# Banded attention and a SiLU layer on one core: batch 2's strided heads turned by VectorE, a subtraction on GpSimd, fewer identity products

## The chip, the cores and the metric

The kernel runs on one core of one Trainium2 chip. Its metric is the device time of one execution, in microseconds (us). A profiled execution also gives a span, from the first to the last instruction, and a trace of every instruction of TensorE (PE), VectorE (DVE), ScalarE (ACT), GpSimd (POOL) and the sync engine's DMA queue (SP).

## The reference

There are 8 batches, 8 heads, 576 positions and 64 numbers per head. Heads 0 to 3 attend to the last 32 positions, heads 4 to 7 to every fourth of the last 128. The result goes, token by token, through two matrices with SiLU between them.

```python
B, H, S, D = q.shape                      # 8, 8, 576, 64
scores = np.matmul(q, k.transpose(0, 1, 3, 2)) / np.sqrt(D)
rel = np.arange(S)[:, None] - np.arange(S)[None, :]
plain = (rel >= 0) & (rel < 32)
dilated = (rel >= 0) & (rel < 128) & (rel % 4 == 0)
scores = np.where(plain or dilated by head, scores, -1e9)
attn = np.exp(scores - scores.max(-1, keepdims=True))
attn = attn / (attn.sum(-1, keepdims=True) + 1e-9)
x = np.matmul(attn, v)                    # to (B * S, H * D) = (4608, 512)
h = x @ w_in                              # (4608, 2048)
out = (h * sigmoid(h)) @ w_out            # (4608, 512), float32
```

## The kernel before

Everything is cut by batch `b` and by kind of head `z`: `z = 0` for the four plain heads, `z = 1` for the four strided ones, whose positions are sorted into four classes (position modulo 4) so that each class is again a plain band. A band is computed in blocks of 32 queries by 64 keys, four heads side by side on the 128 partitions. The steps for one `(b, z)` are these.

- `load_qk` brings q and k on GpSimd's DMA queue into a pair of tiles `n0`, `n1` (a pool with two buffers each, so batch `b + 2` uses the buffers of batch `b`). `load_one` loads rows of many positions; `load_squares` loads in blocks of 32 by 32 or 32 by 96, in more and smaller pieces. For `b >= DT` (3) the squares are used.
- q and k must lie with the 64 numbers of a head on the partitions. Below `DT`, `transpose` (L249) does this with TensorE, into PSUM tiles `t`, and DVE and ACT copy them out (`to_classes` for `z = 1`). From `DT` on, `turn_qk` (L294) does it with one DVE stream transpose each for k and q, from the squares.
- `scores` runs the small products (`score`, `score_class`, `score_turned`) into PSUM, `masked` (L374) adds scale and mask into `ms`, `reduce_max` (L441) gives the negated maxima `nm`. Each half `hi` of the blocks has tiles of its own.
- `exps` (L521) runs on ACT, one pair of instructions for each block of 64 columns: an exponential with the maximum as bias, and the read of its sum into `l`. Where `shift` has already subtracted the maxima, one wide exponential (L510) does it, and `total` (L529) sums on DVE.
- `normal` (L540 to L543) divides on DVE into `pn`, `turned` (L559) turns 32 by 32 blocks into `pt`, `values` (L590) multiplies with `vw`, the v tile, into four PSUM tiles `x`, and `finish` (L622, L624) copies those, as f16, into `xT`.
- `layer1` (L672) multiplies `xT` with `w_in` in 16 steps `f`, each ended by a SiLU on ACT (L680) into `gT`. `layer2` (L741) multiplies `gT` with `w_out` in tiles of 128 tokens, 16 products each, and `store` (L726) copies a tile `o` to SBUF, on DVE, and sends it out on SP's queue.

ScalarE loads a table (1.28 us) whenever it goes from exponentials to SiLU or back.

The order on each engine is the order in which the program issues its instructions; each engine runs its own in that order. `plan_of(b)` lists what of the attention of later batches is issued at which step of batch `b`'s layers: steps 0 to 15 stand ahead of `layer1`'s 16 values of `f`, and from 16 on each step is a quarter (4 products) of a `layer2` tile, so that tile `x` has steps `16 + 4x` to `19 + 4x`. A tile's `store` is issued after its last quarter. `later` lists normalising, values and finish of one `(b, z)` at the steps it is given; during batch `b` the normalising, values and finish of batch `b + 1` are issued.

PSUM has the pool `big` (two buffers, for `h`, `o` and batch 0's scores) and the pool `ps` (four, for all else). An `o` tile waits until the tile two before it has been copied out.

Batch 0 comes ahead of the loop and is done in two parts of its tokens (`part`), each with `scores0`, `values0`, `finish0` and, in the loop, `layer1_part` (L697). `warm` (L632) issues products of the identity with itself, 256 columns wide, whose result is overwritten.

Of the kernel before, what the change touches and what calls it, by code (L numbers as in the profile page):

```python
# [25 lines left out]
DT = 3  # L26
# [3 lines left out]
def kernel(  # L30
# [61 lines left out]
    def tiles_qk(b):  # L92

        for which in (0, 1):
            t = nat.tile([P, GN[0] * QB + GN[1] * GW], F16, tag=f"n{which}", name=f"n{which}_{b}")
            if b >= DT:
                qk[b, 0, which] = t[:, 0 : GN[0] * QB].rearrange("p (g e) -> p g e", e=QB)
                qk[b, 1, which] = t[:, GN[0] * QB :].rearrange("p (g e) -> p g e", e=GW)
                continue
            t = t[:, 0 : 2 * sum(URS) * D].rearrange("p (u d) -> p u d", d=D)  # L100
            u0, u1 = 2 * URS[0], 2 * (URS[0] + URS[1])
            qk[b, 0, which] = t[:, 0:u0].rearrange("p (h u) d -> p h u d", h=2)
            qk[b, 1, which] = t[0 : 2 * UPS[1] if b == 0 else P, u0:u1].rearrange("p (h u) d -> p h u d", h=2)

# [33 lines left out]
    def load_qk(b):  # L138

        tiles_qk(b)  # L140
        if b >= DT:
            for z in (0, 1):
                for which in (1, 0):
                    load_squares(b, z, which)
            return
        for z in (1, 0) if b == 1 else (0, 1):
            for which in (1, 0):
                load_one(b, z, which)
# [182 lines left out]
    def score(b, h, j, dst, start=True):  # L331

        if b >= DT:
            score_turned(b, 0, h, 0, j, dst)
            return
        a = att(b)
        hp = h // 2
        o = (h + hp) % 2 * D
        r = slice(o, o + D)
        nc.tensor.matmul(  # L340
            dst[h * QB : h * QB + QB],
            a["qT"][r, hp, j * QB : j * QB + QB],
            keys(b, a["kT"][r, hp, j * QB : j * QB + KB]),
            start=start,
            stop=True,
            skip_group_check=not start,
        )

    def score_class(b, h, c, j, dst, start=True):

        if b >= DT:
            score_turned(b, 1, h, c, j, dst)
            return
# [93 lines left out]
    def scores(b, z, half=None):  # L447
# [13 lines left out]
        if z:  # L461
            for j in js:
                for c, h in [(c, h) for c in range(DIL) for h in (0, 2, 1, 3)] if b >= DT else [
                    (2 * e + m, h) for e in (0, 1) for h in range(HH) for m in (0, 1)
                ]:
                    e, m = c // 2, c % 2
                    score_class(b, h, c, j, s[m][:, 4 * e + j] if j < 4 else ss[m][:, e])
        else:
            for j in js:
                for h in (0, 2, 1, 3) if b >= DT else range(HH):  # L470
                    score(b, h, j, (*s, ss[0])[j // 8][:, j % 8])
# [144 lines left out]
    def finish(b, z, copy=nc.vector.tensor_copy):  # L616
        a = att(b)
        for e in (0, 1):
            for hp in (0, 1):
                x = a["x", z][e][hp]  # L620
                if z == 0:
# [62 lines left out]
    def layer1_part(f, part):  # L684
# [4 lines left out]
        if part == 0 and f == 0:  # L689
            hs = [ps.tile([P, 2, w], F32, tag="ps", name=f"h_0_{f}_{part}_{x}") for x in (0, 1)]  # L690
            warm(hs[0].rearrange("p n w -> p (n w)"), 4)
# [60 lines left out]
    def transposes(at, b, z, step, copies=both):  # L752
        for which in (1, 0):
            if b >= DT:
# [4 lines left out]
    def later(at, b, z, steps, copy=nc.vector.tensor_copy):  # L759
# [5 lines left out]
        at(steps[3], finish, b, z, copy)  # L765

    def plan_of(b):
# [9 lines left out]
        if b == 0:  # L777
# [21 lines left out]
            later(at, 1, 1, (20, 21, 24, 27), act)  # L799
            later(at, 1, 0, (23, 24, 28, 31), act)  # L800
        elif b == 1:
# [9 lines left out]
            at(20, scores, 3, 0)  # L811
            at(21, exps, 3, 0, 0)
            at(21, exps, 3, 0, 1)
            later(at, 2, 0, (22, 24, 27, 28))
            later(at, 2, 1, (29, 31, 33, 34))
        else:
# [12 lines left out]
            if b + 1 < B:  # L829
                at(12, scores, b + 1, 1)  # L830
                all_exps(b + 1, 1)
                later(at, b + 1, 1, (22, 24, 27, 28))
# [30 lines left out]
    exps(0, 1, 1, 0, 4)  # L863
    turn0(0, 0)
    scores0(0, 1)
    values0(0, 0, 4)
    finish0(0, 0, both)
    exps(0, 1, 1, 4)
# [54 lines left out]
```

## Time and profile before

| what | us |
|---|---|
| median of 3 runs | 309.21 (308.64 to 309.85) |
| the profiled execution | 309.15 |
| its span | 307.2 |
| TensorE busy in it | 294.1 |
| ScalarE busy | 208.3 |
| VectorE busy | 198.1 |
| GpSimd busy | 115.6 |

A line of a timeline gives the start in us from the span's start, the duration in us, the engine, the line of the kernel, the operation, what is written from what, the sizes and how many instructions were merged; in brackets stands the idle time of the engine before it and what ended that. A line of the chain of waits gives start, duration, engine, tile and line; the chain is followed back from the last instruction, at each step to what released it. Matmuls overlap, so merged rows of TensorE end a little after the next row starts.

### The profile page before, as it was taken

How to read it: one execution, taken by the hardware profiler on the slowest of the kernel's cores; microseconds unless marked ns; L12 is line 12 of the kernel's file. 1: busy time of each engine (PE TensorE's matmuls, PEld its weight loads, DVE VectorE, ACT ScalarE, POOL GpSimd, SP SyncE). 2: the span in 40 equal slices, each digit the busy share in tenths (PEclk: the TensorE clock that was granted, in tenths of full speed). 3: DMA queues.
4: the chain of work that ended last, by engine and by line, in shares of the span. 5: the costliest groups of instructions: out<-in, count | busy, mean ns of one | idle time of the engine just before them, and what ended most of it. 6: DMA issues, size and time to landing. Idle time of an engine off the chain costs nothing.

```text
span 307.2 us, 10398 instructions
## 1 busy us (share of the span) xinstructions
PE 294.1 (96%) x4451; PEld 187.7 (61%) x4451; DVE 198.1 (64%) x354; ACT 208.3 (68%) x704; POOL 115.6 (38%) x177
## 2 busy tenths in 40 slices
PE   2899999999999999999999999999999999999995
PEld 2477644577545775477644775478644775478544
DVE  2867579536999768966894768965895762820012
ACT  2588677866999659965795559975796558546200
POOL 8836268859904296235906086150000000000000
PEclk9999999999999999999999999999999999999999
DMA  6999999999993899398969199390011000200021
GB/s 112 174 206 208 206 162 167 190 166 118 115 161 65 91 62 136 111 109 34 124 110 148 40 56 137 108 117 2 2 70 70 34 4 23 80 36 2 11 92 68
DMA packets 107517, 30.18 MB, mean 98 GB/s; under 512 B 90848, under 2 KB 102992, under 8 KB 107472
## 3 DMA queue, kind: packets, MB, share of 16 engines
q0 software_dynamic: 102144, 20.09, 77.6%
q1 hardware_dynamic: 5328, 9.44, 8.4%
q8 instruction: 34, 0.56, 0.8%
q14 instruction: 11, 0.09, 0.1%
HBM read 40.16 MB, written 9.44 MB: 161 GB/s over the span
## 4 chain that ended last, share of the span: by engine, by line
PE 81%; DVE 7%; ACT 7%; issue 2%; DMA 2%; POOL 0%; POOLq 0%
PE h L672 36%; PE o L741 28%; PE o L717 4%; ACT pe L521 4%; PE h L697 4%; PE x L590 4%; PE s L329 2%; DMA n<-in_q_dram 2%; DVE pn L543 1%; DVE ob L726 1%; PE t L276 1%; PE s L340 1%; ACT xT L624 1%; DVE xT L624 1%; ACT gT L705 1%
## 5 line engine op out<-in xcount | busy, mean ns | idle before, releaser
L672 PE MATMUL h<-xT,w_in 128*128 128x288 f16 x896 | 113.9, 286 | 0.2
L680 ACT ACTIVATE gT<-h 128x576 f16<-128x576 f32 x112 | 72.8, 650 | 60.7 <-PE h L672 60.4
L741 PE MATMUL o<-w_out,gT 128*128 128x512 f16 (+1 forms) x528 | 113.8, 373 | 0.0
L672 PEld LDWEIGHTS <-w_in 128*128 128x128 f16 x896 | 86.5, 98 | 24.1 <-issue 0.8
L741 PEld LDWEIGHTS <-gT 128*128 128x128 f16 x528 | 50.7, 98 | 55.4
L521 ACT ACTIVATE pe<-ms,nm 128x64 f32<-128x64 f32 x246 | 81.6, 333 | 0.1
L726 DVE COPY ob<-o 128x512 f32<-128x512 f32 (+1 forms) x35 | 23.1, 660 | 46.7 <-PE o L741 45.2
L521 ACT ACTIVATION_READ_ACCUMULATOR pe<-ms,nm 128x1 f32 x246 | 45.9, 187 | 0.0
L129 POOL DMA_DIRECT2D n<-in_k_dram x40 | 29.3, 748 | 26.0 <-DVE kC L302 25.5
L374 DVE SCALAR_TENSOR_TENSOR ms<-s,mask 128x512 f32<-128x512 f32 x28 | 19.2, 686 | 30.7 <-PE s L329 19.2
L156 POOL DMA_DIRECT2D vw<-in_v_dram x32 | 18.3, 580 | 42.2 <-PE x L590 38.3
L129 POOL DMA_DIRECT2D n<-in_q_dram x40 | 29.4, 754 | 0.5 <-DMA n<-in_q_dram 0.3
L543 DVE TENSOR_TENSOR pn<-pe,r 128x640 f16<-128x640 f32 (+2 forms) x32 | 25.3, 792 | 1.1
L559 DVE STREAM_TRANSPOSE pt<-pn 128x640 f16<-128x640 f16 (+4 forms) x32 | 24.7, 772 | 1.1
L165 POOL DMA_DIRECT2D vw<-in_v_dram x32 | 21.2, 674 | 11.0 <-DMA w_out<-in_moe_w_out_dram 7.6
L441 DVE TENSOR_REDUCE nm<-ms 128x10 f32<-128x640 f32 (+1 forms) x28 | 22.0, 786 | 1.0
L590 PEld LDWEIGHTS <-vw 32*64 32x64 f16 (+1 forms) x1264 | 13.4, 107 | 8.2 <-issue 6.5
L697 PE MATMUL h<-xT,w_in 128*128 128x256 f16 (+1 forms) x128 | 17.2, 288 | 0.0
L590 PE MATMUL x<-pt,vw 32*64 32x64 f16 (+2 forms) x1264 | 15.6, 193 | 1.3 <-DVE pt L559 1.2
L624 DVE CAST xT<-x 128x288 f16<-128x288 f32 x24 | 16.3, 818 | 0.0
L717 PE MATMUL o<-w_out,gT 128*128 128x512 f16 x64 | 14.7, 380 | 0.2 <-ACT ob L726 0.2
L622 DVE CAST xT<-x 128x288 f16<-128x288 f32 x24 | 9.3, 448 | 8.3 <-PE x L590 8.3
(84 smaller groups left out, 213.4 us busy)
## 6 DMA issues: line engine op xcount, KB each, us to landing
out_dram<-ob SPq DMA_DIRECT2D x35, 256.0 KB, 2.1
vw<-in_v_dram POOLq DMA_DIRECT2D x31, 80.0 KB, 3.8
vw<-in_v_dram POOLq DMA_DIRECT2D x32, 72.0 KB, 3.7
n<-in_k_dram POOLq DMA_DIRECT2D x20, 108.0 KB, 3.8
n<-in_q_dram POOLq DMA_DIRECT2D x20, 108.0 KB, 5.0
w_in<-in_moe_w_in_dram POOLq DMA_DIRECT2D x4, 512.0 KB, 9.4
w_out<-in_moe_w_out_dram POOLq DMA_DIRECT2D x4, 512.0 KB, 11.4
n<-in_k_dram POOLq DMA_DIRECT2D x20, 72.0 KB, 3.4
```

Of the source, the lines that this page charges most:

```text
L129: nc.gpsimd.dma_start(out=qk[b, z, which][o : o + QB], in_=bass.AP((q, k)[which].tensor, (b * H + z * HH + half * HH // 2) * S * D + x * Q ...
L521: nc.scalar.activation(pe[:, t, :], src[t], AF.Exp, bias=a["nm", z, hi][:, t : t + 1], scale=k, accum_out=l[:, t : t + 1],)
L543: nc.vector.tensor_tensor(pn[:, 0:w], a["pe", z, hi][:, 0:w], r[:, 0:w, None].broadcast_to([P, w, KB]), ALU.mult)
L559: nc.vector.transpose(out, src)
L590: nc.tensor.matmul(x[h // 2][h % 2 * D : h % 2 * D + D, col : col + wd], vws[b % 2][r, NB + kb * DIL + c if z else kb], turned_cols(b, pt[ ...
L624: copy(a["xT"][:, 2 + hp].rearrange("d (i r) -> d r i", r=DIL)[:, 2 * e : 2 * e + 2], x.rearrange("d (r i) -> d r i", r=2)[:, :, 0:CL],)
L672: nc.tensor.matmul(h[:, half, 0:HS], w_in16[:, c, f * P : f * P + P], xT[:, c, half * HS : half * HS + HS], start=(c == cs[0]), stop=(c == ...
L680: nc.scalar.activation(gT[:, f, s0 : s0 + S].rearrange("p (a c) -> p a c", a=2), h[:, :, 0:HS], AF.Silu)
L697: nc.tensor.matmul(hs[i // m][:, i % m, 0 : c1 - c0], w_in16[:, c, (f + i) * P : (f + i + 1) * P], xT[:, c, c0:c1], start=(c == 0), stop=( ...
L717: nc.tensor.matmul(o, gT[:, f, t * P : (t + 1) * P], w_out16[:, f, :], start=(f == 0), stop=(f == NFF - 1),)
L726: copy(ob, o)
L741: nc.tensor.matmul(o[:, 0, 0:m], gT[:, f, t * P : (t + 1) * P], w_out16[:, f, cols], start=(f == 0), stop=(f == NFF - 1),)
```

## The change

It has five parts.

- **Start.** `warm` runs 2 instead of 4 products before batch 0's values of `(z, part) = (0, 0)` and 3 instead of 4 before its first `layer1_part`. The 12 exponentials of part (1, 1) are issued in one run, where 4 came before the first values of `z = 0` and 8 after. Both `xT` copies of part (0, 0) are on DVE, where one was on ACT.
- **Batch 2's strided q and k.** `DT` becomes a pair, `(3, 2)`, by kind of head: for `z = 1` the squares and DVE's turn begin with batch 2. Its loads become 8 DMAs instead of 4, its 48 TensorE transposes and 4 copies become 2 stream transposes.
- **Batch 3's first maxima.** `shift(3, 0, 0)` on GpSimd, at step 21 of batch 1, after the 16 loads of `load_qk(4)` on that engine's queue. The 8 pairs of exponentials of this half become one exponential of 512 columns, and `normal` gets a `total` on DVE.
- **Batch 2's last copies.** `finish` takes a pair of engines. The four `xT` copies of `(2, 1)` go to DVE and ACT in turn; the others stay where they were.
- **Normalising.** The second half of `(b + 1, 1)` is normalised at step 23 instead of 24 of batch `b`, for `b` from 2 to 6, which puts its four DVE instructions ahead of the copy of `layer2`'s second tile. For batch 2 the step goes from 31 to 30, which leaves DVE's order as it was.

```diff
--- before.py
+++ after.py
@@ -23,7 +23,7 @@
 KB = 2 * QB
 HF = P // 2
 URS = (9, 12)
-DT = 3
+DT = (3, 2)
 
 
 @with_exitstack
@@ -93,14 +93,17 @@
 
         for which in (0, 1):
             t = nat.tile([P, GN[0] * QB + GN[1] * GW], F16, tag=f"n{which}", name=f"n{which}_{b}")
-            if b >= DT:
-                qk[b, 0, which] = t[:, 0 : GN[0] * QB].rearrange("p (g e) -> p g e", e=QB)
-                qk[b, 1, which] = t[:, GN[0] * QB :].rearrange("p (g e) -> p g e", e=GW)
-                continue
+            sq = [
+                t[:, 0 : GN[0] * QB].rearrange("p (g e) -> p g e", e=QB),
+                t[:, GN[0] * QB :].rearrange("p (g e) -> p g e", e=GW),
+            ]
             t = t[:, 0 : 2 * sum(URS) * D].rearrange("p (u d) -> p u d", d=D)
             u0, u1 = 2 * URS[0], 2 * (URS[0] + URS[1])
             qk[b, 0, which] = t[:, 0:u0].rearrange("p (h u) d -> p h u d", h=2)
             qk[b, 1, which] = t[0 : 2 * UPS[1] if b == 0 else P, u0:u1].rearrange("p (h u) d -> p h u d", h=2)
+            for z in (0, 1):
+                if b >= DT[z]:
+                    qk[b, z, which] = sq[z]
 
     def load_one(b, z, which):
 
@@ -138,14 +141,9 @@
     def load_qk(b):
 
         tiles_qk(b)
-        if b >= DT:
-            for z in (0, 1):
-                for which in (1, 0):
-                    load_squares(b, z, which)
-            return
         for z in (1, 0) if b == 1 else (0, 1):
             for which in (1, 0):
-                load_one(b, z, which)
+                (load_squares if b >= DT[z] else load_one)(b, z, which)
 
     def load_v(b):
 
@@ -330,7 +328,7 @@
 
     def score(b, h, j, dst, start=True):
 
-        if b >= DT:
+        if b >= DT[0]:
             score_turned(b, 0, h, 0, j, dst)
             return
         a = att(b)
@@ -348,7 +346,7 @@
 
     def score_class(b, h, c, j, dst, start=True):
 
-        if b >= DT:
+        if b >= DT[1]:
             score_turned(b, 1, h, c, j, dst)
             return
         a = att(b)
@@ -460,14 +458,14 @@
         js = range(0 if half != 1 else cut, cut if half == 0 else n)
         if z:
             for j in js:
-                for c, h in [(c, h) for c in range(DIL) for h in (0, 2, 1, 3)] if b >= DT else [
+                for c, h in [(c, h) for c in range(DIL) for h in (0, 2, 1, 3)] if b >= DT[1] else [
                     (2 * e + m, h) for e in (0, 1) for h in range(HH) for m in (0, 1)
                 ]:
                     e, m = c // 2, c % 2
                     score_class(b, h, c, j, s[m][:, 4 * e + j] if j < 4 else ss[m][:, e])
         else:
             for j in js:
-                for h in (0, 2, 1, 3) if b >= DT else range(HH):
+                for h in (0, 2, 1, 3) if b >= DT[0] else range(HH):
                     score(b, h, j, (*s, ss[0])[j // 8][:, j % 8])
         ms_ = {None: (0, 1), 0: () if z else (0,), 1: (0, 1) if z else (1,)}[half]
         for m in ms_:
@@ -613,11 +611,12 @@
             for c in range(DIL):
                 products(b, z, 0, c, 0, NC, lambda j: (c // 2, xs[c // 2], (c % 2 * NC + j) * QB))
 
-    def finish(b, z, copy=nc.vector.tensor_copy):
+    def finish(b, z, copies=(nc.vector.tensor_copy, nc.vector.tensor_copy)):
         a = att(b)
         for e in (0, 1):
             for hp in (0, 1):
                 x = a["x", z][e][hp]
+                copy = copies[hp]
                 if z == 0:
                     copy(a["xT"][:, hp, e * HS : e * HS + HS], x[:, 0:HS])
                 else:
@@ -688,7 +687,7 @@
         n, w = ((4, SA), (2, 512))[part]
         if part == 0 and f == 0:
             hs = [ps.tile([P, 2, w], F32, tag="ps", name=f"h_0_{f}_{part}_{x}") for x in (0, 1)]
-            warm(hs[0].rearrange("p n w -> p (n w)"), 4)
+            warm(hs[0].rearrange("p n w -> p (n w)"), 3)
         else:
             hs = [big.tile([P, n, w], F32, tag="big", name=f"h_0_{f}_{part}")]
         m = n // len(hs)
@@ -751,18 +750,18 @@
 
     def transposes(at, b, z, step, copies=both):
         for which in (1, 0):
-            if b >= DT:
+            if b >= DT[z]:
                 at(step, turn_qk, b, z, which)
                 continue
             at(step, transpose, b, z, which, copies)
 
-    def later(at, b, z, steps, copy=nc.vector.tensor_copy):
+    def later(at, b, z, steps, copies=(nc.vector.tensor_copy, nc.vector.tensor_copy)):
 
         for hi in (0, 1):
             at(steps[hi], normal, b, z, hi)
             at(steps[hi], turned, b, z, hi)
         at(steps[3], values, b, z)
-        at(steps[3], finish, b, z, copy)
+        at(steps[3], finish, b, z, copies)
 
     def plan_of(b):
         ev = {}
@@ -796,8 +795,8 @@
             all_exps(1, 1)
             for hi in (0, 1):
                 at(20, exps, 1, 0, hi)
-            later(at, 1, 1, (20, 21, 24, 27), act)
-            later(at, 1, 0, (23, 24, 28, 31), act)
+            later(at, 1, 1, (20, 21, 24, 27), (act, act))
+            later(at, 1, 0, (23, 24, 28, 31), (act, act))
         elif b == 1:
             at(16, load_v, 3)
             transposes(at, 2, 0, 3)
@@ -809,10 +808,11 @@
             all_exps(2, 0)
             all_exps(2, 1)
             at(20, scores, 3, 0)
+            at(21, shift, 3, 0, 0, nc.gpsimd)
             at(21, exps, 3, 0, 0)
             at(21, exps, 3, 0, 1)
             later(at, 2, 0, (22, 24, 27, 28))
-            later(at, 2, 1, (29, 31, 33, 34))
+            later(at, 2, 1, (29, 30, 33, 34), both)
         else:
             if b + 2 < B:
                 at(16, load_v, b + 2)
@@ -829,7 +829,7 @@
             if b + 1 < B:
                 at(12, scores, b + 1, 1)
                 all_exps(b + 1, 1)
-                later(at, b + 1, 1, (22, 24, 27, 28))
+                later(at, b + 1, 1, (22, 23, 27, 28))
 
         def plan(s):
             for fn, args in ev.pop(s, ()):
@@ -860,12 +860,11 @@
     scaled(1, 1)
     values0(1, 0, 3)
     finish0(1, 0, (act, act))
-    exps(0, 1, 1, 0, 4)
+    exps(0, 1, 1)
     turn0(0, 0)
     scores0(0, 1)
-    values0(0, 0, 4)
-    finish0(0, 0, both)
-    exps(0, 1, 1, 4)
+    values0(0, 0, 2)
+    finish0(0, 0)
     shift0(0, 1)
     exps(0, 0, 1)
     turn0(1, 1)
```

## The prediction

> **What bounds the kernel now.** I read the page first, then the chain of waits in order of time, then the timelines of TensorE, VectorE (DVE), ScalarE (ACT) and GpSimd (POOL) where the chain leaves TensorE. The page gives the frame:
>
> ```profile
> PE 294.1 (96%) x4451; PEld 187.7 (61%) x4451; DVE 198.1 (64%) x354; ACT 208.3 (68%) x704; POOL 115.6 (38%) x177
> PE h L672 36%; PE o L741 28%; PE o L717 4%; ACT pe L521 4%; PE h L697 4%; PE x L590 4%; PE s L329 2%; DMA n<-in_q_dram 2%; DVE pn L543 1%; DVE ob L726 1%; PE t L276 1%; PE s L340 1%; ACT xT L624 1%; DVE xT L624 1%; ACT gT L705 1%
> ```
>
> TensorE is busy for 294.1 of 307.2 us. The first 5.4 us wait for the first load, the last 3 hold the last copy and store. So little is left to win outside three kinds of place: the start, where TensorE runs on results of other engines; transposes that TensorE need not do; and short waits at the end of a batch. The start, from TensorE's timeline:
>
> ```profile
> 17.60 1.03 PE L632 MATMUL x<-ident 128*128 128x256 f16 x4
> 18.56 0.61 PE L590 MATMUL x<-pt,vw 32*64 32x64 f16 x32
> 19.10 1.03 PE L632 MATMUL h<-ident 128*128 128x256 f16 x4
> 19.93 3.81 PE L697 MATMUL h<-xT,w_in 128*128 128x256 f16 x32
> 24.14 0.69 PE L590 MATMUL x<-pt,vw 32*64 32x32 f16 x64 [0.39 <-DVE pt L559]
> ```
>
> The L632 rows are identity products whose results nobody uses. The wait before 24.14 is for `pt` of batch 0, which hangs on ScalarE:
>
> ```profile
> 19.26 0.37 ACT L663 CAST xT<-x 128x256 f16<-128x256 f32 x1 [0.86 <-PE x L590]
> 21.56 0.35 ACT L521 ACTIVATE pe<-s,nm 128x64 f32<-128x64 f32 x1
> 22.04 0.18 DVE L540 TENSOR_SCALAR r<-l 128x12 f32<-128x12 f32 x1 [1.67 <-ACT pe L521]
> ```
>
> ACT has done 4 of 12 exponentials, then stands 0.86 us for a copy that TensorE has not yet made possible, and DVE waits 1.67 us for the other eight. The chain in the later places:
>
> ```profile
> 70.38 0.70 PE t L276 x48
> ...
> 98.85 0.53 DVE ob L726
> 99.38 0.04 issue
> 99.42 1.14 PE h L672 x8
> 100.56 0.04 issue
> ...
> 127.39 0.27 PE x L590 x20
> 127.66 0.71 PE x L590 x53
> ```
>
> Here are 48 transposes of batch 2, two waits of TensorE as batch 2's layer 1 begins, and a break inside batch 3's `values`.
>
> **Start: fewer identity products, plain exponentials, copies on DVE.** All times here are those of the profile before. The values of part (0,0) followed the fourth L632 by 0.35 us and the third would have come 0.21 after the second (17.60 to 18.56 is 3 x 0.204 + 0.35). With two, values begin at 17.78 + 0.35 = 18.13, after `pt`, whose turn (17.39, 0.45) ends at 17.84; they end 0.43 earlier. Three instead of four L632 for `h` (0.21 each) bring TensorE to its first real product at 19.29. The two `xT` copies now follow each other on DVE (0.42, 0.34 apart by the rows at 19.21 and 19.56): the second ends near 19.55, so the second chunk starts at 19.6 instead of 20.14. In the trace single products of 256 columns start 0.213 us apart until 20.30 and 0.109 apart from then on. If that step stays at its time, five slow products are done by then instead of two: the 32 end at 23.34 instead of 23.58. ACT gains more: 12 exponentials in one run, 0.289 apart from 17.07, end at 20.6 instead of 22.0, so `pt` is ready at 22.7 instead of 24.08 and TensorE does not wait: its values start at 23.34, not 24.13, a gain of 0.79. The next wait, 0.18 before 26.70, goes too: DVE's sum and turn for (0,1) end by 25.3, TensorE comes at 25.7. Together 0.99. What is late next: the fourth quarter of `w_in`, whose landing releases POOL at 25.76; it is needed at 26.2. Between ends I take 0.99; 0.4 if the 20.30 step slides with the work, 1.2 if it comes earlier.
>
> **Batch 2's strided q,k.** TensorE loses the 48 transposes, 0.70 us, all on the chain. DVE loses two copies (0.76, 0.75) and gets two turns; batch 3's rows at L302 are 1.37 and 1.33. DVE ends its reduction at 70.7 and can turn until 73.35. TensorE, without transposes, asks for them 24 products later, 70.38 + 3.05 = 73.43. That is a tie: I charge nothing and put 0.3 in the range. ACT loses two copies of 0.65, nobody waits for them. The 80 score products cost 0.74 either way (L356 0.61 + 0.13, L329 0.61 + 0.14). The loads: four of 0.57 on GpSimd's queue (L116) become eight of 0.65 (2.61 for four at L129), +2.9 us; the packets grow from 384 to 4608. At the mean of queue q0 (77.6% of 16 engines' 307.2 us over 102144 packets, 37 ns) that is 10.7 us of all engines, against 5 us from 46 to 51 before: +2.9 to +5.7. Behind them stand batch 3's loads, landed at about 66 and used at 78.13, batch 2's v, used at 89.0, and batch 4's q,k, used at 115.4. All keep 6 us or more, so this costs nothing but the queue's delay, which matters next.
>
> **GpSimd subtracts batch 3's first maxima.** `pe` of part (3,0,0) then takes one exponential of 512 (0.62, from 0.78 for 640 at 21.85) instead of eight pairs (0.33 each, 2.65): ACT saves 2.0. DVE adds one sum (0.69, as L441's 128x512). The subtraction stands in GpSimd's queue behind batch 4's 16 loads, whose last issue is 82.06 + 2.61 = 84.67 before, so 87.6 to 90.4 now. No row shows its price. The nearest are 0.29 for 128 elements a partition (identity) and 0.26 for 64 (band), so 0.29 to 2.1; I take four times the first, 1.2. It ends at 88.9. The Trainium skill ("GPSIMD Engine Reference", section 3.1) gives 4497 ns for the same operation on 2048 elements; scaled to 512, an estimate of 1.1 us, the sum would be the same. ACT comes to it after 38 exponentials, at 92.5 on the old clock, which is 90.8 with the 1.7 already won. So it is hidden, by 1.9 us.
>
> **Batch 2's last copies on both engines.** `xT` L624 took DVE four times 0.68, and the row at 98.85 is the `ob` copy queued behind them. With two on ACT, DVE reaches `ob` when TensorE has finished it (98.2) and ends at 98.9; TensorE wants it at 99.05. ACT ends its exponentials at 96.5, copies until 97.85, loads its table (1.28) and gives its first `gT` at 99.85; TensorE wants that at 100.03. Both waits go, 0.27 + 0.20 = 0.47. The added sum delays DVE's next `pt` to 103.9; TensorE comes at 104.1.
>
> **Normalising one step sooner**, in batches 3 to 7 (batch 2's move changes no order). `ob` of tile 1 moves behind the second half's normalising:
>
> ```profile
> 124.89 0.65 DVE L726 COPY ob<-o 128x512 f32<-128x512 f32 x1
> 126.76 0.85 DVE L559 STREAM_TRANSPOSE pt<-pn 128x640 f16<-128x640 f16 x1
> 127.32 1.04 PE L590 MATMUL x<-pt,vw 32*64 32x64 f16 x80
> ```
>
> `pt` comes 0.57 earlier, at 127.0, and the wait inside the values goes: 0.16 in each of four batches (single records near 127.5, 160.6, 197.2, 230.3), 0.65. `ob` then ends near 127.65, and tile 3, which needs its buffer, starts at 128.2 after the values. ACT's twentieth exponential (118.22 + 20 x 0.332 = 124.86) is just in time. Before batch 7 `pt` waits for ACT (264.37), so its 0.5 us stays; `ob` there ends at 267.1 and tile 3 starts at 267.2, another tie.
>
> **Sum.** 0.99 + 0.70 + 0.47 + 0.65 = 2.81. The profiled execution took 309.15 us (span 307.2 and 1.95 around it), 0.06 below the median 309.21. 309.15 - 2.81 = 306.34; with 0.05 for the ties 306.4.
>
> **Rivals.**
> *The clock at the start.* The step at 20.30 may fail to come because fewer products run before it. For: three identity products less, 0.64 us. Against: the work that follows moves up, and between 16.9 and 20.3 TensorE stands no longer than before (gaps of about 0.1). If the step were one stretch of 3.4 us later, 16 products at 0.213 would run where 31 ran at 0.109, 1.7 us lost: 308.1. The Trainium skill ("TensorE: Matmul & The Clock Gate", Part 1) says that the clock is released after about 3.4 us of sustained activity in a window that runs freely; the step in the rows fits it, but no run here shows where the window lies. Chance 0.09.
> *The subtraction blocks DVE.* DVE is continuously busy from 81.4 to 99.4, and `pt` of (2,1) reaches TensorE 0.15 late at 95.5. If an operation of DVE stands for the whole 1.2 us of the subtraction, TensorE waits for it: 307.5. Against: where I place the subtraction DVE mostly copies out of PSUM. The Trainium skill ("SBUF — State Buffer", Who interferes with whom) says that a DVE instruction with two SBUF inputs and a reading GpSimd instruction exclude each other; only `pn` is such a one there, and no row here shows the two together. Chance 0.10.
> *The subtraction is late.* It sits last in a queue that carries 2.9 us more. If it must wait until batch 4's loads have landed (DMA traffic ends at about 88 before), at the upper prices it ends at 88.2 + 4.9 + 2.1 = 95.2. ACT stands, and its exponentials, copies and table load reach batch 2's layer 1 late. It decides from 91.0 on, one for one (my first `gT`, 99.85, has 0.2 to spare): +4.2, 310.6, slower than before. Against: GpSimd's issues run without a wait from 66 to 84.7. Chance 0.07.
> *The start gains nothing lasting*: TensorE arrives early at something with a fixed time, a load or its 0.70 us of "issue" near 39. 307.3. Chance 0.08; the loads used up to 42 landed 1 us or more ahead.
>
> **Numbers.** My case has 0.66, with its own range 305.6 to 307.3 (ties +0.5, start -0.2 to +0.6). From 305.5 to 308.2 the range takes in the clock, the block and the lost start, leaving out the late subtraction. A measurement of this kernel can tell about 0.5%, 1.55 us, so faster means under 307.66: nearly all of my case, most of the lost start and the block, 0.76. The same: the clock and the rest of these, 0.17. Slower: the tail of the late subtraction and what I do not see, 0.07.
>
> **What would show it.** Right: no wait of TensorE before its L590 near 23.3; no L276 after the scores of batch 2's first heads; two turns of 1.35 us on DVE there; batch 2's layer 1 starting 1.7 us earlier and running evenly; values of batches 3 to 6 unbroken. Wrong: slow 256-column products beyond 20.5; a gap before the scores near 72; ACT waiting for POOL near 91; DVE multiplying for 2 us instead of 0.83 beside the subtraction.

## The result, and the profile after

| | median us | range | ratio to before (95%) |
|---|---|---|---|
| before, the runs beside it | 308.66 | 308.1 to 309.85 | |
| after | 307.17 | 306.17 to 308.42 | 0.9948 (0.9927 to 0.9969) |

The change is worth 1.5 us between the medians. The two profiled executions stand 2.1 apart in their spans (307.2 and 305.1; 309.15 and 306.95 in all). The forecast was 306.4: it is 0.8 too low, inside its range of 305.5 to 308.2. Every median here is over executions in the faster of two states; only two executions of this study, one of turns at step 6 and one of both, fell in the slower.

The page of the kernel after, the busy line and the chain that ended last:

```profile
PE 292.7 (96%) x4400; PEld 186.9 (61%) x4400; DVE 199.7 (65%) x354; ACT 206.4 (68%) x688; POOL 119.6 (39%) x182
PE h L671 32%; PE o L740 31%; DMA w_out<-in_moe_w_out_dram 5%; DMA n<-in_q_dram 5%; DMA w_in<-in_moe_w_in_dram 4%; PE x L588 3%; ACT pe L519 2%; DMA n<-in_k_dram 2%; PE s L327 2%; POOL n L132 2%; POOL n L112 1%; DMA vw<-in_v_dram 1%; DVE pn L541 1%; POOL w_in L171 1%; DVE ob L725 1%
```

TensorE still fills 96% of the span; it lost 1.4 us of busy time. 51 instructions are gone: 48 transposes and three identity products. Up to 70.53 the chain now runs back through GpSimd's loads, where it ran through TensorE with copies and exponentials between; DVE had no idle time just before that point, so it did not stand for a load there. The start of the kernel after, in the timelines of TensorE, DVE and ACT (start, duration, engine, line, operation):

```profile
18.00 0.61 PE L631 MATMUL x<-ident 128*128 128x256 f16 x2
18.53 0.61 PE L588 MATMUL x<-pt,vw 32*64 32x64 f16 x32
19.07 0.82 PE L631 MATMUL h<-ident 128*128 128x256 f16 x3
19.19 0.76 DVE L662 CAST xT<-x 128x256 f16<-128x256 f32 x2
19.69 5.19 PE L696 MATMUL h<-xT,w_in 128*128 128x256 f16 x32
21.20 0.17 DVE L538 TENSOR_SCALAR r<-l 128x12 f32<-128x12 f32 x1 [0.53 <-ACT pe L519]
22.66 0.58 DVE L557 STREAM_TRANSPOSE pt<-pn 128x384 uint32<-128x384 uint32 x1
24.81 0.69 PE L588 MATMUL x<-pt,vw 32*64 32x32 f16 x64
```

`pt` is ready at 23.24, and TensorE does not come for it before 24.81: the 32 products took 5.19 us where before they took 3.81 (19.93). The wait that was to go is gone, and TensorE arrives later than it did with the wait.

The chain of the kernel after, where it stood on transposes, copies and a break before:

```profile
70.53 1.37 DVE kC L300
71.90 1.27 DVE qC L300
73.17 0.04 issue
73.22 0.68 PE s L327 x62
...
97.40 5.88 PE h L671 x48
103.28 0.77 PE x L588 x75
...
125.98 0.81 PE x L588 x79
```

DVE's two turns stand in the place of the transposes, and TensorE waits for the second one. Batch 2's layer 1 runs in one piece, and so do the values of batch 3.

**Where the 2.1 us of the two profiles are.** I cut both traces on TensorE at three points: the first `values` row, the first product of layer 2 (`o`), and the last product. Each length is a difference of two starts.

| stretch | before | after | difference |
|---|---|---|---|
| span's start to first `values` | 15.19 | 15.58 | +0.40 |
| first `values` to first `o` | 26.53 | 25.96 | -0.57 |
| first `o` to last product | 261.85 | 259.94 | -1.91 |
| last product to the end | 3.60 | 3.60 | 0.00 |

The first row is the fourth load of the start (q of `z = 0`), which landed at 10.80 instead of 10.17; that comes ahead of everything that was changed. The second row is not a gain of the start: the profile before has a stop of 0.87 between twelve and twenty-four transposes at 39 (the distance between two starts, less the usual one; 0.70 in the bracket, "issue"), and no other trace of this study has one of over 0.31 there. Without it the stretch was 25.66, and the changed start lost 0.30. In the third row there are 0.70 of transposes, 0.56 of batch 2's layer 1 (98.07 to 104.61 was 6.54, 97.23 to 103.21 is 5.98), 0.67 of the normalising (0.16 or 0.17 in each of four batches), and 0.35 of a second such stop before (67.6), less the new wait of 0.38 at 73.2: 1.90 of 1.91.

### The profile page after: what moved, and what is told of

Its sections match the earlier page's. It is cut to its first block, busy times and chain, and to the rows that moved or that the text cites. A ratio compares the mean times of both kernels' runs of the same rounds, so it can differ in the third digit from the quotient of the medians.

```text
span 305.1 us, 10290 instructions
## 1 busy us (share of the span) xinstructions
PE 292.7 (96%) x4400; PEld 186.9 (61%) x4400; DVE 199.7 (65%) x354; ACT 206.4 (68%) x688; POOL 119.6 (39%) x182
## 2 busy tenths in 40 slices
DMA packets 111805, 30.47 MB, mean 100 GB/s; under 512 B 95520, under 2 KB 107280, under 8 KB 111760
## 4 chain that ended last, share of the span: by engine, by line
PE 69%; DMA 16%; POOL 5%; DVE 4%; ACT 3%; issue 2%; POOLq 0%
PE h L671 32%; PE o L740 31%; DMA w_out<-in_moe_w_out_dram 5%; DMA n<-in_q_dram 5%; DMA w_in<-in_moe_w_in_dram 4%; PE x L588 3%; ACT pe L519 2%; DMA n<-in_k_dram 2%; PE s L327 2%; POOL n L132 2%; POOL n L112 1%; DMA vw<-in_v_dram 1%; DVE pn L541 1%; POOL w_in L171 1%; DVE ob L725 1%
## 5 line engine op out<-in xcount | busy, mean ns | idle before, releaser
L671 PEld LDWEIGHTS <-w_in 128*128 128x128 f16 x896 | 86.6, 98 | 23.5 <-issue 0.2
L519 ACT ACTIVATE pe<-ms,nm 128x64 f32<-128x64 f32 x238 | 78.9, 333 | 0.1
L519 ACT ACTIVATION_READ_ACCUMULATOR pe<-ms,nm 128x1 f32 x238 | 44.5, 187 | 0.0
L132 POOL DMA_DIRECT2D n<-in_k_dram x44 | 31.9, 736 | 26.2 <-DVE kC L300 25.1
L132 POOL DMA_DIRECT2D n<-in_q_dram x44 | 31.9, 735 | 3.5 <-DMA n<-in_q_dram 3.1
L163 POOL DMA_DIRECT2D vw<-in_v_dram x32 | 21.1, 665 | 9.7 <-DMA w_out<-in_moe_w_out_dram 8.0
L696 PE MATMUL h<-xT,w_in 128*128 128x256 f16 (+1 forms) x128 | 18.6, 302 | 0.0
L696 PEld LDWEIGHTS <-w_in 128*128 128x128 f16 x128 | 12.7, 103 | 3.9 <-issue 0.2
L623 DVE CAST xT<-x 128x288 f16<-128x288 f32 x22 | 15.0, 819 | 0.0
```

What stands on the lines that cost most here:

```text
L132: nc.gpsimd.dma_start(out=qk[b, z, which][o : o + QB], in_=bass.AP((q, k)[which].tensor, (b * H + z * HH + half * HH // 2) * S * D + x * Q ...
L163: nc.gpsimd.dma_start(out=vw[h * QB : h * QB + QB, 0:NB], in_=v[b, h].rearrange("(m p) d -> p m d", p=QB))
L519: nc.scalar.activation(pe[:, t, :], src[t], AF.Exp, bias=a["nm", z, hi][:, t : t + 1], scale=k, accum_out=l[:, t : t + 1],)
L671: nc.tensor.matmul(h[:, half, 0:HS], w_in16[:, c, f * P : f * P + P], xT[:, c, half * HS : half * HS + HS], start=(c == cs[0]), stop=(c == ...
L696: nc.tensor.matmul(hs[i // m][:, i % m, 0 : c1 - c0], w_in16[:, c, (f + i) * P : (f + i + 1) * P], xT[:, c, c0:c1], start=(c == 0), stop=( ...
```

## The experiments

Three theories stood against one another. **Clock:** the start's edits do what they say, but the time at which TensorE's 256-column products go from 0.213 to 0.109 us apart belongs to the execution and not to the work, so what they bring differs from one execution to the next. **Work:** fewer identity products hold that step back. **Block:** GpSimd's subtraction keeps DVE from working, somewhere that the profile after doesn't show. Kernels that were measured together share the runs of the kernel before.

**The four parts alone.** The edits are those of the diff above, one part on the kernel before: the start; `DT = (3, 2)`; the subtraction with batch 2's copies on both engines; the normalising.

> Only the start's edits on the kernel before: two and three identity products for four and four, the 12 exponentials in one run, both xT copies on DVE. In the profile of the whole change the 256-column products of the first layer 1 started 0.213 us apart until 22.7, in the kernel before until 20.3, so the start lost 0.3 us there where 0.99 had been forecast. Window theory (the step to 0.109 falls where a period of the chip's own happens to end, whatever the program does): the step lies anywhere between about 19.5 and 23 from execution to execution, the mean gain is 0 to 0.6 us, ratio 0.998 to 1.000, and the times spread by over 1 us. Work theory (the products taken away hold the step back): the step is at 22 to 23.5 again, no gain or a loss, ratio 1.000 to 1.003. In both, ACT's 12 exponentials end 1.4 us earlier and the wait of 0.66 before the values of part (1,1) is gone.

> Only batch 2's strided q and k as squares, turned by DVE, on the kernel before. Stall theory: DVE finishes its turns 5.6 us after it begins masking batch 2's plain scores, whatever TensorE does; TensorE saves 0.70 us of transposes and stands 0 to 0.55 before the strided scores (0.54 in the whole change, where its 0.18 us of issue amid the plain scores was gone), so the net is 0.15 to 0.70 us, ratio 0.998 to 0.9995. Rival, the loads: the 4224 added packets delay something in the first 45 us or before batch 3's turn at 78, and the net is a loss, ratio above 1.000. Instruction theory of the 0.9 us of issue near 39: it sits at the same instruction as in the kernel before, since nothing ahead of it is changed; noise theory: it is gone or elsewhere.

> Only batch 3's first maxima subtracted on GpSimd and batch 2's last copies on both engines, on the kernel before. Theory: the two waits of 0.27 and 0.20 us at the start of batch 2's layer 1 and the 0.12 before its last chunk go, 0.5 to 0.6 us as in the whole change (0.56), ratio 0.998; GpSimd's subtraction takes 1.05 us and starts about 84.7, 4 us earlier than in the whole change (88.82), and so beside other DVE work: if the two block each other, a DVE multiplication then takes up to 1.8 us instead of 0.83 and the values of (2,1) come up to 1 us late, ratio 1.000 to 1.001; if not, all DVE durations stay within 0.1 us. The issue of 0.9 us near 39: as for the kernel with the turn alone.

> Only the second half's normalising one step sooner, for batches 3 to 7, on the kernel before. Theory: 0.16 us in each of four batches, 0.65 in all, ratio 0.998, with the values of batches 3 to 6 unbroken and batch 7's wait of 0.5 kept. Rival, the buffer: the copy of tile 1, now behind the normalising, holds back tile 3 and gives the gain back, ratio 1.000, with a gap of TensorE after the values in place of the one inside them.

| part alone | median us | ratio (95%) | span of its profile |
|---|---|---|---|
| start | 308.84 | 0.9997 (0.9972 to 1.0023) | 308.7 |
| strided q and k of batch 2 | 308.37 | 0.998 (0.9958 to 1.0002) | 306.6 |
| subtraction and copies | 309.2 | 1.000 (0.9975 to 1.0025) | 306.8 |
| normalising | 307.69 | 0.9963 (0.9942 to 0.9984) | 305.9 |

Only the normalising stands clear of no change, at 1.1 us (0.5 to 1.8); 0.65 was forecast and lies inside. The start alone brings nothing that can be measured. Its profile shows both sides: TensorE's values of part (1,1) come 8.66 us after the first `values`, where before it was 8.95, and the 256-column products stayed slow until 22.93:

```profile
20.92 4.58 PE L697 MATMUL h<-xT,w_in 128*128 128x256 f16 x32
25.43 0.69 PE L590 MATMUL x<-pt,vw 32*64 32x32 f16 x64
```

Its span is long for two reasons that are none of the edit: the first `values` began at 16.77, the second load of the start having landed at 8.27, 1.3 us later than in the kernel after, and the last store took 1.4 us longer than in the other profiles.

The strided part alone has the wait too (0.38 in the bracket before the scores, at 73.38; the expectations count it as 0.54, the distance of two starts less that of two products of layer 1). The subtraction alone took its full gain at 98 (layer 1 of batch 2 is one piece, 98.24 to 104.22, 5.98 us) and gave it back at 88. Timelines of this kernel, DVE, GpSimd and TensorE:

```profile
84.67 1.05 POOL L494 TENSOR_TENSOR ms<-ms,nm 128x512 f32<-128x512 f32 x1
84.93 1.36 DVE L541 TENSOR_TENSOR pn<-pe,r 128x512 f16<-128x512 f32 x1
88.52 0.41 PE L588 MATMUL x<-pt,vw 32*64 32x64 f16 x28
89.73 0.61 PE L588 MATMUL x<-pt,vw 32*64 32x64 f16 x48 [0.79 <-DVE pt L557]
```

Without the eight loads GpSimd is at the subtraction at 84.67, exactly when batch 4's loads ended before. `pn`, 0.69 us elsewhere, takes 1.36 and ends 0.56 after the subtraction: it did its work behind it. All of DVE's row up to `pt` of (2,0) slides by 0.67, and TensorE waits. These two products start 0.98 apart here and 0.31 in the kernels before and after; but the start alone has 0.44 and the strided part 0.62, without any subtraction, so a few tenths of such a wait need not be its work.

**The whole change again, with the DVE turns earlier, with more identity products, and with both.**

```diff
-            transposes(at, 2, 1, 10)
+            transposes(at, 2, 1, 6)       # turns earlier
...
-            warm(hs[0].rearrange("p n w -> p (n w)"), 3)
+            warm(hs[0].rearrange("p n w -> p (n w)"), 4)
...
-    values0(0, 0, 2)
+    values0(0, 0, 4)                      # four and four identity products
```

> The whole change once more, a control. Both clock theories: ratio 0.993 to 0.997, as the nine runs before it. Window theory: the step of the first layer 1 from 0.213 to 0.109 us lies at 20.4 or at 22.6 to 23, as it has done under the unchanged start (20.4 three times, 22.6 once); work theory: again at 22.9. No issue of 0.9 us near 39 and none amid batch 2's plain scores (noise theory) ; the wait of 0.54 before batch 2's strided scores again, since without that issue TensorE comes 0.5 earlier than DVE's second turn ends. GpSimd's subtraction starts at 88 to 89, beside DVE's copies out of PSUM, and no DVE multiplication takes over 0.9 us.

> The whole change with batch 2's two DVE turns issued at step 6 of batch 1 instead of 10, ahead of the masking of batch 2's plain scores, where DVE stands idle for 4.3 us (63 to 67.5). Stall theory: the wait of 0.54 us before the strided scores goes and nothing takes its place, 0.5 us faster than the whole change, ratio to the kernel before 0.992 to 0.995. Rival: batch 2's squares have not landed at 63.5 (their last issue is at 50.9 and the loads behind them crowd the DMA engines), DVE stands with the masking behind it and the gain is lost or turned, ratio 0.995 to 0.998.

> The whole change with four and four identity products again, everything else of the start kept (12 exponentials in one run, both copies on DVE). Work theory: the step is back at 20.4, the first layer 1 then ends 1 us earlier, about 0.6 us faster than the whole change, ratio 0.990 to 0.994. Window theory: the step falls as before, early or late, and the 0.64 us of added products come off the lead: the same or up to 0.4 us slower, ratio 0.994 to 0.998.

> Both edits: the early turns and four and four identity products. The sum of the two: by stall and work theory 1.1 us faster than the whole change, ratio 0.989 to 0.992; by stall and window theory 0.1 to 0.5 us faster, ratio 0.993 to 0.996; by the rivals of both no gain on the whole change.

| kernel | median us | ratio (95%) | span | subtraction at | wait added at 88 |
|---|---|---|---|---|---|
| the change again | 308.04 | 0.9972 (0.9945 to 0.9999) | 306.1 | 86.61 | 1.54 |
| turns at step 6 | 306.45 | 0.9925 (0.9898 to 0.9953) | 305.9 | 86.82 | 1.07 |
| four and four | 307.62 | 0.9966 (0.9939 to 0.9992) | 305.1 | 87.92 | 0.00 |
| both | 306.44 | 0.9915 (0.9881 to 0.9948) | 305.4 | 85.81 | 1.35 |

The last column is the distance between the starts of the 28th and 29th product of `values` (2,0), less the 0.31 that it has in the kernels before and after. Moving the turns took the wait at 73 away: the scores follow at 72.94 with no bracket. Of the edits tried on top of the change it is the one that lowered the median most, by 1.6 us, more than the 0.38 of the wait and the 0.5 that was expected; the two intervals overlap a little, so its size stays open. Four and four identity products on top of it change the median by 0.01 (306.44), where the work theory expected 0.6; on top of the change alone they lower it by 0.4, inside the intervals.

The same program, run again, has what the first profile did not show. The change again, in its timelines, and then the kernel with earlier turns:

```profile
86.17 1.54 DVE L538 TENSOR_SCALAR r<-l 128x10 f32<-128x10 f32 x1
86.61 1.06 POOL L494 TENSOR_TENSOR ms<-ms,nm 128x512 f32<-128x512 f32 x1
88.00 0.82 DVE L541 TENSOR_TENSOR pn<-pe,r 128x640 f16<-128x640 f32 x1
89.75 0.60 PE L588 MATMUL x<-pt,vw 32*64 32x64 f16 x48 [1.66 <-DVE pt L557]
```

```profile
86.67 1.90 DVE L541 TENSOR_TENSOR pn<-pe,r 128x640 f16<-128x640 f32 x1
86.82 1.06 POOL L494 TENSOR_TENSOR ms<-ms,nm 128x512 f32<-128x512 f32 x1
88.61 0.84 DVE L557 STREAM_TRANSPOSE pt<-pn 128x640 f16<-128x640 f16 x1
89.51 0.61 PE L588 MATMUL x<-pt,vw 32*64 32x64 f16 x48 [1.19 <-DVE pt L557]
```

In one an addition over ten columns (`r<-l`, 0.15 us elsewhere) stands until 0.04 after the subtraction; in the other `pn` (0.82) ends 0.69 after it. That short row began 0.44 before the subtraction, and 0.33 before it in the kernel with both (1.50 us), while GpSimd was still issuing loads; what held it in that part is not shown. In the profile after the subtraction ran from 88.82, and DVE did other work:

```profile
88.58 0.65 DVE L725 COPY ob<-o 128x512 f32<-128x512 f32 x1
88.82 1.05 POOL L494 TENSOR_TENSOR ms<-ms,nm 128x512 f32<-128x512 f32 x1
89.16 1.54 DVE L621 CAST xT<-x 128x288 f16<-128x288 f32 x4
```

A copy and casts out of PSUM ran at their usual times (four casts take 1.53 without a subtraction beside them). Nor is every row that reads SBUF held: with four and four a transpose ran its usual 0.84 beside the subtraction (87.83 and 87.92), and with the subtraction ahead of the loads a reduction its usual 0.82 (83.44 and 82.77). So the price of the subtraction is a matter of what DVE holds when GpSimd's queue lets it through, and that moves from 85.8 to 88.8 between executions of nearly the same order, with the landing of the loads ahead of it.

**The subtraction elsewhere, or not at all; the start without identity products, or as before.** All four have the turns at step 6.

```diff
-            at(17, load_qk, 4)
...
             at(21, shift, 3, 0, 0, nc.gpsimd)
+            at(22, load_qk, 4)            # the subtraction ahead of the loads
```

```diff
-            at(21, shift, 3, 0, 0, nc.gpsimd)
-            later(at, 2, 1, (29, 30, 33, 34), both)
+            later(at, 2, 1, (29, 31, 33, 34))   # loads where they were, no tail
```

The third and fourth have the subtraction ahead of the loads, and no identity product ahead of batch 0's parts, or the start of the kernel before in all its edits.

> The early turns, and batch 4's 16 loads issued after GpSimd's subtraction instead of ahead of it (step 22 instead of 17). Block theory (while GpSimd subtracts, a DVE operation that reads SBUF only stands: 1.90 for 0.82, 1.54 for 0.15 in the runs so far): the subtraction now starts when its maxima are there, near 82, beside masking that reads PSUM, no DVE operation is stretched, TensorE waits 0.3 us before the values of (2,0) instead of 0.3 to 1.85, and the times lie closer together: ratio 0.988 to 0.991, about 0.9 us below the early turns alone. Rival: the subtraction meets another DVE operation there, or batch 4's loads, now 8 to 11 us later, are missed by their turn at 113: ratio 0.992 or more, with a long DVE row near 83 or a wait for a load near 113.

> The early turns without the tail: batch 3's first maxima are taken off by ACT's eight pairs as in the kernel before, and batch 2's last copies are all on DVE. Block theory: nothing is stretched, the wait before the values of (2,0) is 0.3, and the two waits of 0.27 and 0.20 and the 0.12 at the start of batch 2's layer 1 are back: ratio 0.990 to 0.993, 0.5 us slower than with the subtraction ahead of the loads and no slower than the early turns with the subtraction behind them. Rival (the subtraction's place does not matter): 0.5 us slower than both.

> The subtraction ahead of the loads, and no identity products at all before the values of (0,0) and before the first layer 1 (0 and 0 for 2 and 3; the three before the values of (1,0) stay). Work theory: TensorE works 1 us less in the stretch before, the step from 0.213 to 0.109 comes at 23 or later, and the first layer 1 ends 0.5 us later or more: ratio 0.5 us or more above the same with 2 and 3. Window theory: the step lies between 20.3 and 23 as in all runs so far, the first product is earlier by what the copies let it, at most 0.3 us, and the time is the same within 0.5 us.

> The subtraction ahead of the loads and the early turns, with the start of the kernel before. Window theory: the start's edits are worth 0.2 us with a late step and up to 1 with an early one, so this is 0.2 to 0.8 us slower than the same with the new start. Work theory: the new start keeps the clock low longer and the old one is the same or up to 0.5 us faster.

| kernel | median us | ratio (95%) | span |
|---|---|---|---|
| subtraction ahead of the loads | 306.98 | 0.994 (0.9918 to 0.9962) | 305.4 |
| no tail | 307.28 | 0.9946 (0.9924 to 0.9967) | 304.4 |
| no identity products there | 307.38 | 0.996 (0.9941 to 0.9979) | 305.8 |
| start as before | 307.08 | 0.9941 (0.9919 to 0.9962) | 304.7 |

Ahead of the loads the subtraction runs from 82.77 (from 82.0 to 83.2 in the three kernels that have it so), and the block is gone: `pn` keeps 0.82. What is left is small in the trace. The median does not show it: 0.9 us less than with turns at step 6 was expected, but this kernel has 306.98 beside 308.67 for the kernel before, that one 306.45 beside 308.79. What the block costs on average over many executions is therefore not shown. The subtraction ahead of the loads, timelines:

```profile
82.77 1.04 POOL L494 TENSOR_TENSOR ms<-ms,nm 128x512 f32<-128x512 f32 x1 [5.66 <-DVE nm L439]
83.75 3.23 POOL L132 DMA_DIRECT2D n<-in_k_dram  x4
84.18 0.38 DVE L538 TENSOR_SCALAR r<-l 128x8 f32<-128x8 f32 x1
87.28 0.82 DVE L541 TENSOR_TENSOR pn<-pe,r 128x640 f16<-128x640 f32 x1
89.03 0.61 PE L588 MATMUL x<-pt,vw 32*64 32x64 f16 x48 [0.40 <-DVE pt L557]
```

The wait at 88 is 0.29 over the usual distance, from two short DVE rows that are longer beside GpSimd's loads (0.38 and 0.23 for 0.16 and 0.15) and because TensorE arrives without its wait at 73. From the first `o` to the last product this kernel takes 259.82 us; without the tail it is 260.07; the whole change again, with its block, 261.49. So by these single traces the tail is worth some 0.25 where its subtraction blocks nobody, and costs where it does. The medians, 306.98 and 307.28, are in that order (0.5 was expected between them), but their intervals do not part them.

**The start, over all traces.** For every profile I took three starts on TensorE: the first real product of `layer1_part` (L696 or L697), the start of the first product that follows 0.109 behind another, and the values of part (1,1). "Slow for" is the second less the first; "to values (1,1)" counts from the first `values`. (So the prediction's 20.30, where the last slower distance ends, is 20.41 here.)

| start | kernel | step at | slow for | to values (1,1) |
|---|---|---|---|---|
| before | before | 20.41 | 0.48 | 8.95 |
| before | subtraction and copies | 20.43 | 0.10 | 8.95 |
| before | normalising | 20.36 | 0.11 | 8.95 |
| before | start as before | 20.97 | 0.72 | 8.94 |
| before | strided part | 22.59 | 2.27 | 9.40 |
| after | turns at step 6 | 21.16 | 0.78 | 8.08 |
| after | subtraction ahead | 20.45 | 0.42 | 8.32 |
| after | no tail | 20.93 | 1.39 | 8.36 |
| after | start alone | 22.93 | 2.01 | 8.66 |
| after | the change again | 22.03 | 2.50 | 8.88 |
| after | after | 22.97 | 3.28 | 9.23 |
| after, four and four | both | 20.95 | 0.91 | 8.35 |
| after, four and four | four and four | 22.01 | 1.38 | 8.94 |
| after, none | no identity products | 24.82 | 5.39 | 10.24 |

The old start takes 8.94 or 8.95 four times out of five, with steps up to 20.97: it waits for `pt`. The new start takes what the slow products leave it: each microsecond of them costs 0.49 (0.104 lost for each product of 0.213), which leads from 8.36 with 1.39 to 9.29 with 3.28, measured 9.23. (The kernel with the subtraction ahead also waited for `w_in` there: two of its products start 0.53 apart instead of 0.11.) The step itself comes by 20.36 at the earliest and at 22.97 at the latest in the thirteen executions with identity products. (In the two rows with 0.10 and 0.11 the real products are fast from the first on, and the four identity products ahead of them take 0.86 and 0.94 us instead of 1.03: the step lies among these, near 20.2.) In the profiles with the start as in the kernel after, all alike up to there, it comes between 20.45 and 22.97, with no relation to when the work began: first `values` at 15.92 and 15.58 in those two. That is what the clock theory says. The work theory is not needed for two or three products fewer, and with four and four the step was not back at 20.4, as it expects, but at 22.01 and 20.95; with none at all, the only execution profiled stepped 1.85 later than any other:

```profile
19.43 6.21 PE L695 MATMUL h<-xT,w_in 128*128 128x256 f16 x32 [0.61 <-DVE xT L662]
25.56 0.69 PE L588 MATMUL x<-pt,vw 32*64 32x32 f16 x64
```

One execution does not show it, and the medians (307.38 against 306.98) stay within their intervals. The Trainium skill ("TensorE: Matmul & The Clock Gate", Part 1) says that the window of about 3.4 us runs freely and that one kernel therefore has more or fewer slow products from run to run; the spread of 2.6 us or more over thirteen executions agrees. An estimate by that page's figure puts the step without identity products one window behind a usual one, 24.82 - 3.4 = 21.4; that a window was not filled there, one execution does not show.

## Why the prediction was right, and where it was not

The time was forecast on the right side and 0.8 us low. The steps, in the prediction's order:

- **Start, 0.99: failed.** Every edit did what it was said to do. ACT's twelve exponentials run 0.289 apart and end at 21.1, `pt` is ready at 23.24 (22.7 was forecast, on a first `values` 0.40 earlier; the two gains named, 0.79 and 0.18, make 0.97), both copies take 0.76 on DVE, TensorE is at its first product 4.10 after the first `values` instead of 4.74, as forecast, and the waits before 24.14 and 26.70 are gone. What failed is the sentence "If that step stays at its time, five slow products are done by then instead of two". The step was at 22.97: 3.28 us of slow products, fifteen. Ten more than five cost 10 x 0.104 = 1.04; with the 0.40 of the late load that makes the forecast -0.79 a +0.65, and +0.67 was measured (24.14 to 24.81). The rival "The clock at the start", with 0.09, had the place and nearly the price (16 products, 1.7 us), but put it down to the work that is left out; the runs show that the step's time changes among kernels that are alike up to there. The single profile before happened to have the earliest kind, and I read it as the kernel's. Its wait for `pt` was in truth the cover of a late step: the old start loses only 0.45 to a step at 22.59. Over all profiles, without stops like the one at 39, the stretch from the first `values` to the first `o` is 25.83 on average with the old start (25.66, 25.77, 25.83, 25.77, 26.13) and 25.37 with the new one (25.96, 25.39, 25.62, 24.84, 25.14, 25.29): 0.46, not 0.99. To the values of (1,1) the averages of the table are 9.04 and 8.59, which says the same. The medians show less, and nothing clear of noise: with the new start and the old, all else alike, 306.98 and 307.08 (0.2 to 0.8 was expected), and 0.18 for the start alone.
- **Transposes, 0.70: right, with the tie lost.** The two turns took 1.37 and 1.34 (1.37 and 1.33 were taken). "That is a tie: I charge nothing and put 0.3 in the range" came out at 0.38. Earlier turns take this wait away.
- **Loads and GpSimd's queue: right.** Packets went from 107517 to 111805, and the last of batch 4's loads was issued by 88.81 instead of 84.67, inside the 87.6 to 90.4 given. Nobody waited for a late load.
- **The subtraction: size right, cover only half right.** 1.05 us for 1.2, ended at 89.88, and ACT came to it at 91.68, hidden by 1.8 where 1.9 was said. The Trainium skill ("GPSIMD Engine Reference", section 3.1), scaled to an estimate of 1.1 us, agrees. But "The subtraction blocks DVE", with 0.10 and 307.5, is real, and delays the values of (2,0) by 0.67 to 1.54 in four of the six profiles in which the subtraction stands behind batch 4's loads; the profile after is one of the other two. The rule drawn on there, of the Trainium skill ("SBUF — State Buffer", Who interferes with whom), agrees with `pn`'s 0.69 to 1.36 and 0.82 to 1.90. "Only `pn` is such a one there" was too narrow: `r<-l`, with one SBUF input, stood for 1.54 and 1.50. The same section of the Trainium skill names `tensor_scalar`, the form of that row, among those that can contend too.
- **Batch 2's last copies, 0.47: right.** 0.56 in the profiles; in that of the part alone the block takes it all back (0.67), and its ratio is 1.000.
- **Normalising, 0.65: right.** 0.67, at the four places given; batch 7's wait stays. The DVE order after has both `ob` copies behind `pt`:

```profile
124.03 0.82 DVE L541 TENSOR_TENSOR pn<-pe,r 128x640 f16<-128x640 f32 x1
124.89 0.84 DVE L557 STREAM_TRANSPOSE pt<-pn 128x640 f16<-128x640 f16 x1
125.66 1.25 DVE L725 COPY ob<-o 128x512 f32<-128x512 f32 x2
```

- **The late subtraction and the lost start.** GpSimd never kept ACT waiting. "The start gains nothing lasting", 307.3 with 0.08, comes nearest to the measured 307.17 in its number, though for the clock's reason and not for a load's or the stop's at 39. That stop did not come back: among thirteen other traces the longest of its kind, measured as the 0.87 was, are 0.31 at 38.5 (no tail), and 0.64 and 0.93 (turns at step 6, and the subtraction ahead of the loads). These two stand behind the same product, which starts at 27.10 in both; what held TensorE there is open.

With the start at 0.46 instead of 0.99, and 0.38 for the tie, the sum would be 0.46 + 0.70 - 0.38 + 0.47 + 0.65 = 1.90, against 1.5 and, in the second measurement, 0.75 between the medians. Blocks in some of the executions would take part of the rest; how often they come, no untraced run can tell. That the time fell inside its range all the same is owed to the range's width of 2.7 us and to the other gains; the start had no part in it as forecast.

The five versions with earlier turns and identity products (ratios 0.9915 to 0.9946) all lie lower than the change's two measurements (0.9948 and 0.9972), and below the kernel before with their whole intervals; but these overlap with the change's, and which of the five is best, the runs do not part. By the traces I would take the one with the subtraction ahead of the loads, which has neither the wait at 73 nor the block, though its median is not the lowest.

## What to carry to other kernels

A time that one trace shows for something the program does not set, such as a clock step or a load's landing, is one draw: before you move work up against it, ask what the edit is worth if it comes two microseconds later, and whether the wait you remove was its cover. When GpSimd gets arithmetic on SBUF, place it by what DVE does beside it, and put it ahead of the loads in its queue rather than behind, where their landing decides when it runs. Two turns that just fit are a wait: start them a step or two earlier if nothing stands behind them.

## What was not expected of the hardware

- Beside a GpSimd subtraction of 1.05 us not only a two-input DVE operation was held but a ten-column one with one SBUF input: 0.15 became 1.54 and 1.50 us. A transpose (0.84) and a reduction (0.82) were not. Beside GpSimd's DMA issues the same short rows took between their usual 0.15 and 0.40.
- The step from 0.213 to 0.109 us between products came anywhere from about 20.2 to 22.97 in executions of nearly the same start.
- The first `values` began between 15.19 and 16.77 in fourteen profiles, and one last store took 1.4 us longer. Such things, outside what was changed, are as large as the whole gain.
